# Experts' rows and results turned by VectorE in 32x32 blocks, and three five-way branches an expert

## The chip, the cores and the metric

The kernel runs on one core of one Trainium2 chip. The core has a matrix engine (TensorE, PE in the profile, its weight loads PEld), three engines that work on tiles (VectorE or DVE, ScalarE or ACT, GpSimd or POOL) and SyncE (SP), which here only issues transfers. A tile in SBUF has 128 partitions; products land in eight PSUM banks of 512 float32 columns. The metric is the device time of one execution in microseconds (us); lower is better.

## What is computed

```python
# delta rule: B, H, S, D = 4, 8, 768, 48
for t in range(S):
    kt, vt, bt = (k_n[:, :, t], v[:, :, t], beta[:, :, t, None])
    y[:, :, t] = np.einsum('bhd,bhde->bhe', q[:, :, t], state)
    v_old = np.einsum('bhde,bhd->bhe', state, kt)
    state = state + bt[:, :, :, None] * np.einsum('bhd,bhe->bhde', kt, vt - v_old)
...
x = y.transpose(0, 2, 1, 3).reshape(3072, 384)
# experts: E = 8, F = 1024
expert_idx = token_ids * np.int64(2654435761) % np.int64(E)
for e in range(E):
    mask = expert_idx == e
    h = np.maximum(x[mask] @ w1[e], 0.0)
    out[mask] = h @ w2[e]
```

`k_n` is `k` divided by its norm. All inputs and results are float32. The ids of this case give the eight experts 364, 389, 385, 423, 360, 376, 420 and 355 rows.

## The kernel before

**First phase.** The sequence is cut into 24 chunks of 32 steps (`NU`). VectorE inverts a triangular matrix for four chunks at a time (`invert`, L527 and L529), TensorE carries the state from chunk to chunk (`ks`, `ys`, `w`, `s`, `ym`), ScalarE empties PSUM. The finished rows go to `x_scratch` in DRAM with `store_x`, on SP's queue. On the same queue `spread_t` distributes the inverse to a block-diagonal tile `TB`; `spread_m`, on GpSimd's queue, does so for `MB`. The order of all work is written out by hand: `inv.do(us)` and `route.do(us)` let a generator of small VectorE operations run on for about so many microseconds between two steps, and `route.products()` lets it emit its PE products.

**Routing** (`routing`, a generator) runs beside the last eight chunks. It counts ranks with two products (L277, L278), gives every row a slot, compares slots with all positions (`hi`, `lo`, `hv`) and finds with 24 products (L382) which row sits in which slot: `gx` holds row numbers for reading, `gidx` for writing, `wid_i` for each expert which of five widths (360, 376, 392, 408, 424) holds its rows.

**Second phase.** For each expert, `gather` (an indirect transfer on GpSimd's queue, L104) fetches four tiles of 106 rows. `turn` transposes each with three products against the identity and a copy. `gemm1` forms the eight blocks of 128 hidden columns from three products each, `gemm2` the three blocks of 128 output columns from eight each. `put` transposes the result back in four pieces (L925), copies it and scatters it (L929). A float32 product is two passes of PE, so the profile counts two instructions for each.

The widths enter through a switch: `choose` (L875) branches on PE into one of five bodies that differ in the number of rows alone. An expert has two: `rows` over the first four blocks of `gemm1`, and `cols` over the whole `gemm2`. Between them lie the fifth block at the full 424 rows, 24 transposes (the results of the expert before and the rows of the one after) and the last three blocks at 424 rows. A switch can be announced ahead (`hint`, L954): `cols` is announced before the transposes, `rows` right after `cols` of the expert before. Expert 0 has no switch.

```python
                gemm1(i, xT, h_sb, arms[e], range(4), f"rows{e}")
                if e + 1 < E:
                    arms[e + 1] = arm(e + 1)
                gemm1(i, xT, h_sb, ALL, range(4, 5))
                if e + 1 < E:
                    hint(e, "cols")
```

`arm` (L950) loads the next expert's width into a register of PE. For the first expert the rows of the first 21 chunks (`x_early`) are gathered while the last chunks still run: three tiles of rows (`KE = 3`) early, the fourth when all rows are stored. Weights: expert 0's on ScalarE's queue, those of 1 and 2 on GpSimd's, later ones on SP's. A loop over overflow blocks at the end has no iteration with these ids.

Of the kernel before, what the change touches and what calls it, by code (L numbers as in the profile page):

```python
# [19 lines left out]
def kernel(  # L20
# [25 lines left out]

    KT = 4
    KE = 3
    TS = 106
    TD = 112  # L50
    CAP = KT * TS
# [9 lines left out]
    x_early = x_dram[0:CE * C * B]  # L61
# [7 lines left out]
    gx = keep.tile([P, NHI], I32)  # L69
    ov_i = keep.tile([P, NOV + 1], I32)  # L70
# [8 lines left out]
    def load_w(e, eng, i=None, dyn=None):  # L79

        i = e % 3 if dyn is None else i
        s1 = moe_w1[e] if dyn is None else moe_w1[bass.ds(dyn, 1)].rearrange("o d f -> (o d) f")
        s2 = moe_w2[e] if dyn is None else moe_w2[bass.ds(dyn, 1)].rearrange("o f d -> (o f) d")
        for co in range(CO):
            yield
            eng.dma_start(out=W1s[i][:, co], in_=s1[co * P:(co + 1) * P])
        for fo in range(0, FO, 2):
            yield
            eng.dma_start(out=W2w[i][:, fo:fo + 2],
                          in_=s2[fo * P:(fo + 2) * P].rearrange("(o p) d -> p o d", p=P))  # L90
# [12 lines left out]
    def gather(src, idx, xg):  # L103
        nc.gpsimd.indirect_dma_start(  # L104
            out=xg[0:TD], out_offset=None, in_=src,
            in_offset=bass.IndirectOffsetOnAxis(ap=idx[0:TD], axis=0),
            bounds_check=src.shape[0] - 1, oob_is_err=False)
# [10 lines left out]
    with ExitStack() as phase1:  # L118
# [101 lines left out]
        def routing():  # L220
# [12 lines left out]
            for b in range(B):  # L233
# [10 lines left out]
            nc.gpsimd.memset(cont[:, :, 0:1], 0.0)  # L244
            iota_f = rt.tile([P, P], F32)
# [51 lines left out]
                            scalar2=float(KE * TS), op0=ALU.mult, op1=ALU.add)  # L297
# [11 lines left out]
            for n in WIDTHS[1:-1]:  # L309
# [17 lines left out]
                            scalar2=float(E * KT * P - CAP - (KT - 1) * (P - TS)), op0=ALU.mult,  # L327
                            op1=ALU.add)
# [8 lines left out]
            yield 0.65  # L337
            slot = rt.tile([P, NTC], F32)
            V.tensor_reduce(slot, rank.rearrange("p e c -> p c e"), axis=AX.X, op=ALU.add)

            yield 1.0
            col = rt.tile([P, NTC], F32)
            V.tensor_scalar(out=col, in0=slot, scalar1=float(TS), scalar2=None, op0=ALU.is_ge)
            for i in range(2, KT):
                V.scalar_tensor_tensor(out=col, in0=slot, scalar=float(TS * i), in1=col,
                                       op0=ALU.is_ge, op1=ALU.add)
            V.scalar_tensor_tensor(out=slot, in0=col, scalar=float(P - TS), in1=slot,
                                   op0=ALU.mult, op1=ALU.add)
# [32 lines left out]
            for i in range(NTC):  # L381
# [11 lines left out]
            V.scalar_tensor_tensor(out=gx, in0=row, scalar=-1.0, in1=none, op0=ALU.add,  # L393
                                   op1=ALU.add)

            yield 1.2
            row_p = rt.tile([P, 3, NHI], I32)
# [9 lines left out]
            V.tensor_tensor(gidx, row, none, op=ALU.add)  # L407
# [128 lines left out]
        class Work:  # L536

            def __init__(self, it):
                self.it = it
                self.next = next(it, None)  # L540
                self.owed = 0.0

# [8 lines left out]
            def products(self):  # L551
                if self.next == "PE":
                    self.next = next(self.it, None)
# [233 lines left out]
        rt = rt_stack.enter_context(tc.tile_pool(name="rt", bufs=1, side="right"))  # L787
        w_parts = load_w(0, nc.scalar)
# [3 lines left out]
        xg0 = [XTs[1][:, i * DIN:i * DIN + DIN] for i in range(KT)]  # L792
        for c in range(NU - 2 * GC, NU + 1):
            first, last = c == NU - 2 * GC, c % GC == GC - 1
            if c < NU:
                if not last:
# [6 lines left out]
            if c < NU:  # L803
# [6 lines left out]
                if c == NU - 3:  # L810
                    route.do(3.0)
                elif c == NU - 2:
                    route.do(None)
                w(c, 0)
                if c == NU - GC:
                    assert route.next == "PE"
                    route.products()
# [5 lines left out]
            if c < NU:  # L823
# [5 lines left out]
                if c == NU - 2:  # L829
                    assert route.next == "PE"  # L830
                    route.products()
                ym(c, 0)
                y_out(c, 0)
                inv, us = invert_b(c)
                inv.do(us)
                if c >= NU - GC - 1:
                    route.do(None if c >= NU - 2 else 2.0 if c < NU - GC else 4.0)
                w(c, 1)
            if c == NU - 2:
                for kt in range(KE):  # L840
                    gather(x_early, gx[:, kt:kt + 1], xg0[kt])
# [4 lines left out]
    with tc.tile_pool(name="m_xg", bufs=8) as m_xg, \  # L846
         tc.tile_pool(name="m_h", bufs=2) as m_h, \
         tc.tile_pool(name="m_y", bufs=1) as m_y, \
         tc.tile_pool(name="m_o", bufs=5) as m_o:

        xTs = [t[:, :CO * CAP].rearrange("p (c n) -> p c n", c=CO) for t in XTs]

        yTs = [m_y.tile([P, CO, CAP + TD - TS], F32, name=f"yT{i}") for i in range(2)]
        for t in yTs:
            nc.vector.memset(t[:, :, CAP:], 0.0)
# [5 lines left out]
        ROWS = [4, 5, 6, 7, 0, 4, 5, 6]  # L861
        COLS = [7, 2, 3]
        ALL = slice(0, CAP)

        def copy(eng, out, in_):
            (nc.scalar.copy if eng is nc.scalar else nc.vector.tensor_copy)(out, in_)  # L866

        def turn(xg, xT, col, width, kt, eng):
            xT_ps = banks[2 + kt % 2][:, :CO * P].rearrange("p (c n) -> p c n", c=CO)
            for co in range(CO):  # L870
                nc.tensor.transpose(xT_ps[:, co, :width], xg[:width, co * P:(co + 1) * P],  # L871
                                    ident[:width, :width])
            copy(eng, xT[:, :, col:col + width], xT_ps[:, :, :width])

        def choose(cols, name):  # L875
# [3 lines left out]
            else:  # L879
                for i in tc.Switch({mybir.EngineType.PE: cols}, len(WIDTHS), hint=name):  # L880
                    yield slice(0, WIDTHS[i])

        def gemm1(i, xT, h_sb, cols, fos=range(FO), name=None):
            for part in choose(cols, name):
                for fo in fos:
                    for co in range(CO):
                        nc.tensor.matmul(banks[ROWS[fo]][:, part],  # L887
# [3 lines left out]
                    if part is cols:  # L891
                        relu(h_sb, fo, cols)
            if part is not cols:
                for fo in fos:
                    relu(h_sb, fo, ALL)

        def relu(h_sb, fo, cols):
            h, h_ps = h_sb[:, fo, cols], banks[ROWS[fo]][:, cols]
# [5 lines left out]
        def gemm2(i, h_sb, yT, cols, cos=range(CO), name=None):  # L904

            def take(co, part):
                copy((nc.scalar, nc.vector)[co % 2], yT[:, co, part], banks[COLS[co]][:, part])

            for part in choose(cols, name):
                for co in cos:  # L910
                    for fo in range(FO):
                        nc.tensor.matmul(banks[COLS[co]][:, part],  # L912
                                         lhsT=W2w[i][:, fo, co * P:(co + 1) * P],
                                         rhs=h_sb[:, fo, part], start=(fo == 0),
                                         stop=(fo == FO - 1))
                    if part is cols:
                        take(co, part)
            if part is not cols:
                for co in cos:
                    take(co, ALL)  # L920

        def put(yT, col, width, idx, kt, alone, eng):
            o_ps = banks[1 - kt % 2]
            for co in range(CO):
                nc.tensor.transpose(o_ps[:width, co * P:(co + 1) * P], yT[:, co, col:col + width],  # L925
                                    ident)
            o_sb = m_o.tile([P, DIN], F32, name="o_sb")
            copy(eng, o_sb[:width], o_ps[:width, :DIN])
            scat = nc.gpsimd.indirect_dma_start(  # L929
                out=out[:, :], out_offset=bass.IndirectOffsetOnAxis(ap=idx[:width], axis=0),  # L930
                in_=o_sb[:width], in_offset=None, bounds_check=N - 1, oob_is_err=False)
# [4 lines left out]
        xgs = {(0, kt): xg0[kt] for kt in range(KT)}  # L936

        def fetch(e):
            for kt in range(KT):
                xgs[e, kt] = m_xg.tile([P, DIN], F32, name="xg")  # L940
                gather(x_dram, gx[:, e * KT + kt:e * KT + kt + 1], xgs[e, kt])

        def turn_one(e, kt):
            turn(xgs.pop((e, kt)), xTs[e % 3], kt * TS, TS, kt, (nc.scalar, nc.vector)[kt % 2])

        def put_one(e, kt):
            put(yTs[e % 2], kt * TS, TD, gidx[:, e * KT + kt:e * KT + kt + 1], kt, True,
                (nc.vector, nc.scalar)[kt % 2])
# [5 lines left out]
        def hint(e, name):  # L954
            tc.switch_hint({mybir.EngineType.PE: arms[e]}, len(WIDTHS), f"{name}{e}")

        def new_h():
            return m_h.tile([P, FO, CAP], F32, name="h_sb")


        gather(x_dram, gx[:, KE:KT], xg0[KE])
        for kt in range(KE):
            turn_one(0, kt)
        for _ in load_w(1, nc.gpsimd):
            pass

        for i in range(8):
            nc.vector.memset(m_xg.tile([P, DIN], F32, name="xg"), 0.0)
        fetch(1)
        for _ in load_w(2, nc.gpsimd):  # L970
            pass


        arms = {}
        for e in range(E):
            h_sb, i, xT = new_h(), e % 3, xTs[e % 3]
            if e == 0:
                gemm1(i, xT, h_sb, slice(0, KE * TS))
                arms[1] = arm(1)
                turn_one(0, KE)  # L980
                gemm1(i, xT, h_sb, slice(KE * TS, CAP))
# [86 lines left out]
```

## Time and profile before

| what | us |
|---|---|
| three runs | 566.9, 995.24, 563.8 |
| their median | 566.9 |
| the profiled execution | 566.48 |
| its span | 564.9 |
| granted clock, mean | 0.938 |
| PE from 300 to 520 us | 219.7 of 220 busy |
| VectorE from 300 to 520 us | 30.6 of 220 busy |

The profiled execution is 1.6 us longer than its span and stands 0.4 us below the median. One of the three runs was far off the other two.

How to read the page: part 1 gives busy time, share of the span and number of instructions for each engine. Part 2 cuts the span into 40 equal slices of 14.1 us; each digit is the busy share in tenths, and the clock row gives the share of full speed granted to PE. The chain that ended last names, from each instruction back, what released it. A line such as `341.39 1.97 PE psK L887 x6` in it gives start, duration, engine, tile, source line and count. "issue" is time in which an engine waited for nothing that the profile shows. A name with a trailing q (`PEldq`, `SPq`) is the engine's sequencer or queue.

### The profile page before, as it was taken

The page shows a single profiled execution, that of the slowest core. Times are in us where ns is not written, and L with a number is a line of the kernel's source. Part 1 is how long each engine was busy: PE and PEld are TensorE (multiplying, and loading weights), DVE is VectorE, ACT ScalarE, POOL GpSimd, SP SyncE. Part 2 cuts the span into 40 slices and gives each one's busy share as a digit, 9 for nine tenths or more (in the row PEclk, how much of TensorE's full clock was granted, in tenths as well). Part 3 has the DMA queues.
Part 4 walks back from the last instruction along what each step waited for, and adds up shares of the span by engine and source line. Part 5 has one row for each costly group of instructions (what it writes and reads, how often), then busy time and mean ns, then how long its engine had stood idle before and what let it go on. Part 6 is the DMA issues. An engine that isn't in the chain of part 4 may idle for free.

```text
span 564.9 us, 14221 instructions
## 1 busy us (share of the span) xinstructions
PE 516.4 (91%) x5596; PEld 385.8 (68%) x5596; DVE 264.9 (47%) x707; ACT 205.7 (36%) x448; POOL 255.9 (45%) x409
## 2 busy tenths in 40 slices
PE   8969798889898878988999999999999999999993
PEld 7858788888788777976675656555566565655572
DVE  6899987998989988396310201102011020200200
ACT  5857575887787523353110202102011020200100
POOL 9608676878878785673672320504105020110202
PEclk9659897999999977599999999999999999999998
DMA  6926576888688495574698153631436310010101
GB/s 107 183 56 102 105 144 112 148 133 157 123 153 147 75 177 121 110 167 103 214 364 242 43 158 112 193 119 54 150 115 192 124 44 3 11 34 3 48 0 40
DMA packets 130282, 66.22 MB, mean 117 GB/s; under 512 B 112856, under 2 KB 120114, under 8 KB 130176
## 3 DMA queue, kind: packets, MB, share of 16 engines
q1 hardware_dynamic: 113328, 33.12, 28.3%
q0 software_dynamic: 15328, 28.39, 20.3%
q10 hardware_dynamic: 1520, 3.15, 1.8%
q8 instruction: 85, 1.39, 1.1%
q14 instruction: 21, 0.17, 0.1%
HBM read 49.67 MB, written 10.22 MB: 106 GB/s over the span
## 4 chain that ended last, share of the span: by engine, by line
PE 51%; issue 0%; ACT 0%; DVE 0%; POOL 0%; POOLq 0%
PE psT L912 15%; PE psS L887 9%; PE psS L912 8%; PE psK L887 6%; PE psW L887 6%; PE psG L887 3%; PE psT L871 2%; PE psG L925 1%; PE psY L925 1%; POOL out_dram L929 0%; ACT xT L866 0%; PE psG L629 0%; PE psG L599 0%; DVE o_sb L866 0%; ACT h_sb L900 0%
## 5 line engine op out<-in xcount | busy, mean ns | idle before, releaser
L929 POOL DMA_INDIRECT out_dram<-o_sb,gidx x32 | 30.5, 953 | 203.7 <-DVE o_sb L866 179.1
L912 PE MATMUL psT<-h_sb,w 128*128 128x424 f32 (+5 forms) x288 | 88.8, 466 | 0.0
L912 PEld LDWEIGHTS psT<-h_sb,w 128*128 128x128 f32 x288 | 52.3, 190 | 35.1 <-issue 15.9
L175 POOL DMA_DIRECT2D K<-in_k_dram x96 | 55.6, 585 | 43.1 <-PE psS L618 36.1
L529 DVE TENSOR_TENSOR U<-U,tmp 128x31 f32<-128x31 f32 (+15 forms) x186 | 63.8, 343 | 6.4
L527 DVE TENSOR_TENSOR tmp<-U,Ni 128x31 f32<-128x31 f32 (+15 forms) x186 | 63.4, 341 | 5.3
L563 POOL DMA_DIRECT2D MB<-MT x96 | 55.5, 584 | 4.4 <-PE psG L629 1.3
L181 POOL DMA_DIRECT2D V<-in_v_dram x96 | 55.5, 584 | 3.4 <-DMA V<-in_v_dram 1.8
L887 PE MATMUL psS<-xT,w 128*128 128x424 f32 (+5 forms) x162 | 52.2, 467 | 0.0
L606 PE MATMUL psW<-R,TB 128*64 128x48 f32 x736 | 35.0, 237 | 13.1 <-DVE R L591 6.9
L464 PE MATMUL psG<-sd,w 96*64 96x64 f32 x640 | 30.4, 245 | 17.3 <-ACT sd L443 11.8
L618 PE MATMUL psS<-W,K 128*96 128x96 f32 x368 | 44.1, 267 | 1.2 <-ACT W L612 1.2
L912 PE MATMUL psS<-h_sb,w 128*128 128x424 f32 (+5 forms) x144 | 45.1, 466 | 0.0
L612 ACT ACTIVATE W<-psW 64x192 f32<-64x192 f32 x96 | 31.2, 324 | 36.1 <-PE psW L606 34.7
L451 ACT ACTIVATE w<-psT,own 96x512 f32<-96x512 f32 x66 | 43.2, 689 | 0.4
L887 PEld LDWEIGHTS psS<-xT,w 128*128 128x128 f32 x162 | 29.5, 190 | 19.9 <-issue 10.9
L866 DVE COPY yT<-psT 128x424 f32<-128x424 f32 (+2 forms) x9 | 5.0, 551 | 80.7 <-PE psT L912 80.7
L618 PEld LDWEIGHTS psS<-W,K 128*96 128x96 f32 x368 | 39.2, 179 | 3.0 <-ACT W L612 1.4
L606 PEld LDWEIGHTS psW<-R,TB 128*64 128x64 f32 x736 | 30.0, 151 | 15.7 <-DVE R L591 10.4
L464 PEld LDWEIGHTS psG<-sd,w 96*64 96x64 f32 x640 | 26.0, 156 | 20.9 <-ACT sd L443 14.8
L912 PEld LDWEIGHTS psS<-h_sb,w 128*128 128x128 f32 x144 | 26.2, 190 | 17.8 <-issue 9.1
L887 PE MATMUL psK<-xT,w 128*128 128x424 f32 (+5 forms) x108 | 36.6, 475 | 1.5 <-DVE xT L866 0.7
(203 smaller groups left out, 795.6 us busy)
## 6 DMA issues: line engine op xcount, KB each, us to landing
w<-in_moe_w_dram SPq DMA_DIRECT2D x15, 512.0 KB
w<-in_moe_w_dram SPq DMA_DIRECT2D x20, 384.0 KB
Kd<-in_k_dram SPq DMA_DIRECT2D x24, 192.0 KB
Qd<-in_q_dram SPq DMA_DIRECT2D x24, 192.0 KB
K<-in_k_dram POOLq DMA_DIRECT2D x96, 48.0 KB, 2.9
V<-in_v_dram POOLq DMA_DIRECT2D x96, 48.0 KB, 3.6
x_scratch<-x_sb SPq DMA_DIRECT2D x96, 48.0 KB
TB<-TU SPq DMA_DIRECT2D x96, 32.0 KB
```

The costliest lines, as they stand in the source:

```text
L175: nc.gpsimd.dma_start(out=K4s[c % 3][quarter(i), :, i % 2, :], in_=k_r[i, c * C:(c + 1) * C])
L181: nc.gpsimd.dma_start(out=Vs[c][quarter(i)], in_=v_r[i, c * C:(c + 1) * C])
L451: nc.scalar.activation(to[:, :, :, r], psT, ACT.Copy, scale=own[:, r:r + 1])
L464: nc.tensor.matmul(psG[pair(p), hg, j, ks], lhsT=KT[:, j, hg, p].rearrange("p r s -> p (r s)"), rhs=sd[:, j, ks, 2 * hg + p], start=True, ...
L527: V.tensor_tensor(tmp, U[:, j:j + 1, 0:n].to_broadcast([P, m, n]), Ni[:, j, j + 1:, None].to_broadcast([P, m, n]), op=ALU.mult)
L529: V.tensor_tensor(U[:, j + 1:, 0:n], U[:, j + 1:, 0:n], tmp, op=ALU.add)
L563: eng.dma_start(out=dst[quarter(i), :, i, :], in_=src[quarter(i)])
L606: nc.tensor.matmul(psW[pair(p), i], lhsT=TBs[c % 2][:, HT * h + i, 2 * p:2 * p + 2].rearrange("k r t -> k (r t)"), rhs=Rs[h][:, i], start= ...
L612: nc.scalar.activation(Ws[h][pair(p), :, p], psW[pair(p)], ACT.Copy)
L618: nc.tensor.matmul(psS[h][:, i], lhsT=K4s[c % 3][:, HT * h + i], rhs=Ws[h][:, i], start=(c == 0 and i == 0), stop=True, skip_group_check=True)
L887: nc.tensor.matmul(banks[ROWS[fo]][:, part], lhsT=W1s[i][:, co, fo * P:(fo + 1) * P], rhs=xT[:, co, part], start=(co == 0), stop=(co == CO ...
L912: nc.tensor.matmul(banks[COLS[co]][:, part], lhsT=W2w[i][:, fo, co * P:(co + 1) * P], rhs=h_sb[:, fo, part], start=(fo == 0), stop=(fo == ...
```

## The change

- **Rows in quarters.** A row of 384 values becomes four quarters of 96. Partition `32*a + j` of a tile holds quarter `a` of the row in place `j` of a 32-row block. VectorE's transpose, which turns every 32x32 block in place, then gives the operand of `gemm1` directly, and one more turns each output block back. For that the weights are read differently: W1 with input `3*p + c` on partition `p`, W2 with every third column (`co::CO`).
- **Where the rows come from.** Experts 1 to 7: `fetch` gathers four whole tiles of 128 rows, `spread_rows` rearranges them with 16 small transfers on SP's queue, `rows_in` turns all 14 blocks with one instruction. Expert 0: 14 gathers of quarters (`KE = 9` blocks early, five late), with indices `x4`.
- **Results.** `rows_out` turns the three PSUM banks and issues 14 scatters of quarters with indices `g4`, in place of four scatters of rows. The last expert's results are still transposed by PE, in four pieces, of which two follow the last product.
- **Three switches an expert**: `top` (blocks 0 to 3), `low` (4 to 7) and `cols`; all are announced inside `choose`, directly ahead. Expert 0 has `cols` too. PSUM banks go round in turn (`take_banks`).
- **Routing** drops the three-step column count, adds two groups of four small products (`by_quarter`), and is spread over chunks 17 to 22: its first products come at the end of chunk 19 and not in chunk 20, its second after `w(22, 0)`.
- **Queues.** Weights of experts 1 and 2 move from GpSimd's to SP's queue. `spread_t` of chunk 17 is issued ahead of the loads of the ids.

```diff
-    KE = 3
-    TS = 106
-    TD = 112
-    CAP = KT * TS
+    KE = 9
+    T = 32
+    QD = DIN // 4
+    CAP = 424
+    NB = -(-CAP // T)
...
-            eng.dma_start(out=W1s[i][:, co], in_=s1[co * P:(co + 1) * P])
+            eng.dma_start(out=W1s[i][:, co], in_=s1.rearrange("(p c) f -> c p f", c=CO)[co])
...
+            yield "PE"
+
+            def by_quarter(idx, n):
+                ps = bank(ps_t, "t")[:, :4 * n].rearrange("p (m k) -> p m k", m=4)
+                for m in range(4):
+                    nc.tensor.matmul(ps[:, m], lhsT=sel[:, m].rearrange("p a j -> p (a j)"),
+                                     rhs=idx[:, 0:n], start=True, stop=True)
+                return ps.rearrange("p m k -> p k m")
+
+            ps = by_quarter(gx_f, KT)
+            yield 0.2
+            V.tensor_scalar(out=x4, in0=ps, scalar1=4.0, scalar2=quarter_f[:, 0:1], op0=ALU.mult,
+                            op1=ALU.add)
...
+        spread_t(NU - 2 * GC + 1)
         w_parts = load_w(0, nc.scalar)
...
-                if c == NU - 3:
-                    route.do(3.0)
-                elif c == NU - 2:
-                    route.do(None)
+                if c >= NU - GC:
+                    route.do(3.5 if c < NU - 2 else None)
                 w(c, 0)
-                if c == NU - GC:
-                    assert route.next == "PE"
-                    route.products()
+                if c == NU - 2:
+                    route.products(2)
...
             if c == NU - 2:
-                for kt in range(KE):
-                    gather(x_early, gx[:, kt:kt + 1], xg0[kt])
+                for m in range(KE):
+                    gather(x_early, x4.rearrange("p k m -> p (k m)")[:, m:m + 1], xq0[:, m])
+                route.products(4)
...
             if isinstance(cols, slice):
                 yield cols
             else:
+                tc.switch_hint({mybir.EngineType.PE: cols}, len(WIDTHS), name)
                 for i in tc.Switch({mybir.EngineType.PE: cols}, len(WIDTHS), hint=name):
                     yield slice(0, WIDTHS[i])
...
+        def rows_in(xT, xq, ms):
+            nc.vector.transpose(
+                xT[:, :, T * ms.start:T * ms.stop].rearrange("p c (m j) -> p m c j", j=T),
+                xq[:, ms].rearrange("p m (i c) -> p m c i", c=CO))
+
+        def rows_out(e, ps):
+            oq = m_o.tile([P, NB, QD], F32, name="oq")
             for co in range(CO):
+                nc.vector.transpose(oq[:, :, co::CO],
+                                    ps[co][:, :CW].rearrange("p (m j) -> p m j", j=T))
+            for m in range(NB):
+                scatter(out_quarters, g4[:, e].rearrange("p k m -> p (k m)")[:, m:m + 1],
+                        oq[:, m])
...
+        def spread_rows(e):
+            xqs[e] = m_xq.tile([P, KT * 4, QD], F32, name="xq")
+            xg = xgs.pop(e)
+            to = xqs[e].rearrange("p (k m) f -> p m k f", m=4)
+            for m in range(4):
+                n = len(range(m, NB, 4))
+                for a in range(4):
+                    nc.sync.dma_start(out=to[T * a:T * a + T, m, :n],
+                                      in_=xg[T * m:T * m + T, :n, QD * a:QD * a + QD])
...
             if e == 0:
-                gemm1(i, xT, h_sb, slice(0, KE * TS))
-                arms[1] = arm(1)
-                turn_one(0, KE)
-                gemm1(i, xT, h_sb, slice(KE * TS, CAP))
+                gemm1(i, xT, h_sb, slice(0, KE * T), range(FO))
+                arms[0] = arm(0)
+                rows_in(xT, xq0, late)
+                gemm1(i, xT, h_sb, slice(KE * T, CAP), range(FO))
             else:
-                gemm1(i, xT, h_sb, arms[e], range(4), f"rows{e}")
-                if e + 1 < E:
-                    arms[e + 1] = arm(e + 1)
-                gemm1(i, xT, h_sb, ALL, range(4, 5))
-                if e + 1 < E:
-                    hint(e, "cols")
-            if e + 2 < E:
-                fetch(e + 2)
-
-            for kt in range(KT):
-                if e > 0:
-                    put_one(e - 1, kt)
-                if e + 1 < E:
-                    turn_one(e + 1, kt)
+                rows_out(e - 1, done.pop(e - 1))
+                gemm1(i, xT, h_sb, arms[e], range(4), f"top{e}")
+            if e + 1 < E:
+                arms[e + 1] = arm(e + 1)
             if e > 0:
-                gemm1(i, xT, h_sb, ALL, range(5, FO))
+                if e + 2 < E:
+                    fetch(e + 2)
+                gemm1(i, xT, h_sb, arms[e], range(4, FO), f"low{e}")
             if e + 1 < E:
-                if e == 0:
-                    gemm2(i, h_sb, yTs[0], ALL)
-                else:
-                    gemm2(i, h_sb, yTs[e % 2], arms[e], name=f"cols{e}")
-                hint(e + 1, "rows")
+                rows_in(xTs[(e + 1) % 3], xqs.pop(e + 1), slice(0, NB))
+                done[e] = take_banks(CO)
+                gemm2(i, h_sb, arms[e], done[e], name=f"cols{e}")
```

## The prediction, made before the changed kernel was run

> **What bounds the kernel now.** I read, in this order: busy shares and slices of the page, the chain that ended last, the sequencer's records of line 1063 (the dispatch of each switch), the granted clock by stretch, GpSimd's timeline at the seam of the two phases.
>
> ```profile
> PE 516.4 (91%) x5596; PEld 385.8 (68%) x5596; DVE 264.9 (47%) x707; ACT 205.7 (36%) x448; POOL 255.9 (45%) x409
> PE   8969798889898878988999999999999999999993
> PEclk9659897999999977599999999999999999999998
> ```
>
> From about 268 us (slice 19 on) TensorE (PE) is never idle: the expert phase costs exactly what PE is given. The chain for expert 2 (its first four blocks, one full-width block, the transposes, the other three):
>
> ```profile
> 341.39 1.97 PE psK L887 x6
> ...
> 349.29 2.14 PE psG L887 x6
> 351.43 0.33 PE psY L925 x3
> ...
> 353.79 0.27 PE psT L871 x3
> 354.06 2.16 PE psK L887 x6
> ```
>
> So 24 PE transposes lie in the chain from 351.43 to 354.06, 2.63 us, and each later block is charged at 424 rows: 2.13 us, where the arm of 392 takes 1.97.
>
> What covers a branch decides the rest. The sequencer's dispatches, of all switches, then entry, exit and the second entry of expert 2:
>
> ```profile
> L1063 PEldq COMPARE_BRANCH  x26: 305/2412/4424, 300.8 to 519.0; - x26
> L1063 PEldq COMPARE_BRANCH  x1: 3807/3807/3807, 336.6 to 336.6; - x1
> L1063 PEldq COMPARE_BRANCH  x1: 3508/3508/3508, 343.2 to 343.2; - x1
> L1063 PEldq COMPARE_BRANCH  x1: 404/404/404, 354.2 to 354.2; - x1
> ```
>
> Columns are minimum, median and maximum in ns and first and last start. The entry of `rows`, hinted just before, holds the sequencer 3.8 us (336.6 to 340.4); leaving that short body takes 3.5 us; the entry of `cols`, hinted 6 us earlier, 0.4 us. PE doesn't notice the first, because the sequencer runs about 5 us ahead (336.6 against the end of the matrix product at 341.39). Once it does:
>
> ```profile
> 446.09 0.27 issue
> 446.36 2.15 PE psK L887 x6
> ```
>
> That entry took 4.42 us. And what an idle PE costs, two stretches of the first phase:
>
> ```profile
> 205.00:218.00 13.00, 11.81 (x166) 11.19 (x168) 10.36 (x27) 2.94 (x8) 7.18 (x13) 0.50 0.60 118
> 225.00:239.00 14.00, 12.88 (x164) 11.85 (x164) 5.19 (x18) 3.59 (x10) 8.57 (x15) 0.51 0.56 109
> ```
>
> The seventh figure is the granted clock, 0.50: PE's own timeline has an idle 2.59 us up to 205.88 and 2.79 us up to 226.12.
>
> [...] the instruction queue moved 85 packets of 1.39 MB (16 KB each), and entries hinted only just before cost 2.1 us (first arm) to 4.4 us. [...] No operand of the kernel before shows a 12-byte stride into PE. [...] the trace has one of 1024 elements at 1.23 us (L500), 1.99 with a strided output (L532).
>
> **Part by part**, against the profiled execution's 566.5 us (span 564.9; the median shown is 566.9, so no correction).
>
> *PE transposes leave.* Experts 1 to 6: 6 x 2.64 (351.43 to 354.06 and its like) = 15.8. Expert 7: 526.78 to 529.03, waits included, 2.25. Expert 0's are in the seam below. Gain 18.1.
>
> *Widths.* From the arms in the trace (392, 392, 424, 360, 376, 424, 360 for experts 1 to 7) blocks 4 to 7 save 4 x (2.13 - 1.98, 1.98, 2.13, 1.81, 1.89, 2.13, 1.81): 0.6+0.6+0+1.3+1.0+0+1.3 = 4.8. Expert 0's second product goes to its arm, 376 by the reference's ids: 48 passes x (0.356 - 0.316) = 1.9. The last one, split 256+168 instead of 324+100: a pass costs 0.84 ns a row (318 rows: 0.267), but 100 rows cost 0.110, a floor; 48 x (0.2725 + 0.110 - 0.215 - 0.141) = 1.3. Gain 8.0.
>
> *Routing and the seam.* Order on VectorE: the first work moves under chunks 17 to 19, whose VectorE wait (idle 5.70 before 240.20) swallows it; the four `lo` compares (3.56) move ahead of chunk 22. The slots' 24 products start some 2.5 us earlier, but then come four small products and one more VectorE step, so I find the first index about where it is:
>
> ```profile
> 258.96 1.09 POOL L104 DMA_INDIRECT xT<-x_scratch,gx  x1 [3.00 <-DVE row_p L398]
> ...
> 272.26 0.99 POOL L104 DMA_INDIRECT xT<-x_scratch,gx  x1 [9.58 <-issue]
> ```
>
> Instead of three gathers nine follow, one every 1.33 us (start to start): the ninth starts at 269.4, lands 3.0 later (median for xT), VectorE turns 864 elements in 1.1: first product at about 273.3, where it now starts at 268.08. PE's last chunk ends near 267: idle 6 us, clock halved. The five late gathers (from 272.3: the last lands at 281, turned by 282) stay under the first 11.6 us product. Both products: 48 x (288 rows 0.242 + 136 rows 0.114) = 17.1, so expert 0's second product begins at 290.4, against 289.39 now: loss 1.0, before the clock. A bound on both sides: an index 3 us earlier gives -2, later +5. Moving `spread_t` ahead of the id loads on SP removes a 1 us wait for TB at 206; the VectorE queue holds R until 205 all the same: gain 1.0.
>
> *Moved off PE at no cost, and their cover.* VectorE: one turn of 1344 elements (1.6 to 2.6) and three of 448 from PSUM (0.5 to 0.9 each) an expert, beside four relus of 0.6: under 8 of 32 us. Its relus queue behind the three output turns, but these are over 3 us into an 8 us block. GpSimd: 14 scatters instead of 4, at 1.25 each 17.5, then four gathers (5.3): 23 of 32 us. SP: 16 spreads at 0.61 = 9.8, behind gathers that land 7 us after issue, and weights behind them; the rows are due a whole expert later. First time tightest: rows for expert 1 turned near 306, due near 314. If that cover is gone, PE waits the difference.
>
> *The new branch.* `low` stands right behind `top`: leaving `top`, loading the next width and entering `low` lie in one line, with only `top`'s 8 us to cover them. Expert 2 with the durations shown: left at 346.7, width and registers to 348.05, dispatch at 348.4, entry 3.8: 352.3, but `top` ends at 349.29: PE idle 3.0. The same sum for experts 1 to 7, arm for arm (first arm 2.1 to 2.4; the others 3.8 to 4.4): 3.1, 3.0, 1.6, 2.1, 4.6, 0, 1.1 = 15.5. `low` to `cols`, which loses its early hint, without the width load: 2.3, 2.2, 0.9, 1.3, 4.1, 0 = 10.8. Expert 0 into its new switch: behind passes of 0.114 the sequencer is 1.8 us ahead, needs 5.7: 3.9. Loss 30.2.
>
> *The clock.* Halved stretches after the start lasted 3.4 us (61.5 to 64.9), 6.8 (88.8 to 95.6) and twice over 13 (above), 9.4 in the mean; half of it is lost: 4.7 us each. Idle of 2 us or more is likely at the seam and in experts 0, 1, 2, 5, perhaps 4: 5.7 of them, 26.8; a halved PE then covers the second entry: -7. Loss 19.8, between 0 (clock held) and 32 (all at 6.8).
>
> *Tail.* Two scatters instead of one after the last product, 1.25 apart: loss 1.3.
>
> Sum: 566.5 - 18.1 - 8.0 + 1.0 - 1.0 + 1.3 + 30.2 + 19.8 = 591.7: **592 us**.
>
> **Unknown both ways:** weights at a 12-byte stride in the second product. A load takes 190 ns under passes of about 330: unseen at up to 1.7 times, +19 us if doubled (50 ns x 48 x 8), a gain excluded since it adds no bandwidth. I take nothing.
>
> **Rivals.** (1) *Entries stay hidden*, because `low`'s first arm lies just behind the exit and its block is already there: no stall, no halving after the seam. 591.7 - 30.2 - 19.8 + 4.7 (the seam's halving stays) = 546, faster. For it: the exits of `cols` cost 0.3 us. Against: entering `rows` right behind such an exit cost 2.1 to 4.4 every time. It turns where exit, width and entry together fall under 8 us. (2) *Stalls, but the clock holds*: 572, range 565 to 578. For it: one slice at 0.63 busy was not punished; against: the two stretches above. (3) *Weight loads bind as well*: 592 + 19 = 611. That the change is not what it says is excluded: the order of instructions shows three switches an expert and no transposes in experts 0 to 6.
>
> **Numbers.** Forecast 0.57 (578 to 606), hidden entries 0.13, clock holds 0.21, weight loads or a later seam 0.09. The range 563 to 612 leaves out the hidden case and the far end. A measurement of this kernel tells about 2% (11 us): faster 0.13, same 0.20 (most of the second rival), slower 0.67.
>
> **What would show it.** Right: idle PE named issue between two L923 groups and before L945, entries of 2 to 4.4 us twice an expert, clock near half in slices of the expert phase, first L923 near 273. Wrong: entries under 0.5 us, PE idle nowhere after 275, or a clock of 1.0 throughout; a weight load over 300 ns would make the third rival.

## The result and the profile after

| | median, us | range, us | executions | profiled, us | span, us | granted clock |
|---|---|---|---|---|---|---|
| before | 565.35 | 560.28 to 995.24 | 4 | 566.48 | 564.9 | 0.938 |
| after | 608.3 | 605.56 to 613.91 | 4 | 605.56 | 604.0 | 0.915 |

The ratio, which leaves out the one execution of 995.24 us, is 1.0805, 95% interval 1.0675 to 1.0934: the change makes the kernel slower. The forecast was 592 in a range of 563 to 612.

The page of the kernel after, the same rows as were shown of before:

```profile
PE 506.9 (84%) x5432; PEld 397.9 (66%) x5432; DVE 278.2 (46%) x700; ACT 186.3 (31%) x405; POOL 327.5 (54%) x479
PE   7967988988988698979788688899969968999990
PEclk9569899999999958879889799898979979999996
```

PE has 164 instructions fewer and is busy 9.5 us less, in a span that is 39.1 us longer. From slice 19 on the row of PE was all nines before; now sixes to eights stand among them, and the clock row dips beside them. So the time went into idle PE and half clock, not into work. The sequencer's records of all switches, then top entry, top exit, `low` entry, `low` exit and `cols` entry of expert 2 (ns minimum, median, maximum; first and last start):

```profile
L1121 PEldq COMPARE_BRANCH  x42: 310/3358/6647, 288.9 to 562.3; - x42
L1121 PEldq COMPARE_BRANCH  x1: 6186/6186/6186, 352.0 to 352.0; - x1
L1121 PEldq COMPARE_BRANCH  x1: 3325/3325/3325, 360.5 to 360.5; - x1
L1121 PEldq COMPARE_BRANCH  x1: 3555/3555/3555, 365.5 to 365.5; - x1
L1121 PEldq COMPARE_BRANCH  x1: 3582/3582/3582, 371.3 to 371.3; - x1
L1121 PEldq COMPARE_BRANCH  x1: 4254/4254/4254, 375.8 to 375.8; - x1
```

That is 21 us in branches within 28 us (352.0 to 380.1). The trace's instruction queue moved ten blocks of 16 KB in that time, one or two of them in each of the five branches, and at least one in each of the 31 branches over 2 us of the whole trace (112 blocks in all, 85 before); a branch of this length is called a fetch below. What PE makes of it, in its own timeline of that expert (start, duration, operation; in brackets the idle time before it and what released it):

```profile
358.48 4.19 PE L923 MATMUL psS<-xT,w 128*128 128x392 f32 x12 [1.63 <-DVE oq L959]
...
364.48 2.14 PE L923 MATMUL psY<-xT,w 128*128 128x392 f32 x6
369.23 4.21 PE L923 MATMUL psT<-xT,w 128*128 128x392 f32 x12 [2.61 <-issue]
...
375.25 2.14 PE L923 MATMUL psW<-xT,w 128*128 128x392 f32 x6
380.31 2.01 PE L945 MATMUL psS<-h_sb,w 128*128 128x392 f32 x4 [2.91 <-issue]
```

Three stalls, one for each entry. The first is put down to VectorE, but the entry that began at 352.0 and took 6.19 us ended at 358.2, just ahead of the block, while VectorE's last turn there ended at 357.7: it is a fetch too. Stalls over 0.7 us between 292 and 568 us, summed by the entry that they stand at: `top` 3.9 (experts 1, 2), `low` 19.6 (experts 1 to 5, 7), `cols` 12.4 (experts 1, 2, 4, 5), 35.9 together, and 3.12 more at expert 0's `cols`. The clock, in three stretches (the columns are the length, then busy time of PE, PEld, DVE, ACT and POOL, the granted clock, the share of DMA and GB/s):

```profile
352.00:359.00 7.00, 5.37 (x17) 3.68 (x17) 1.18 (x2) 0.00 (x0) 0.99 (x1) 1.00 1.02 364
446.25:453.10 6.85, 4.18 (x7) 2.52 (x8) 0.00 (x0) 0.18 (x1) 5.02 (x7) 0.50 0.16 56
482.00:489.00 7.00, 0.58 (x2) 0.38 (x2) 0.60 (x1) 0.00 (x0) 5.31 (x6) 0.87 0.99 360
```

The second is one of seven halved stretches of the expert phase (four of 3.4 us, three of 6.8: 34 us, half of it lost: 17 at most, since PE stood idle in 5 of the 34). The first and third are the two entries of over 6 us in experts 2 and 5: the DMA share was 1.02 and 0.99 while the sequencer fetched. That was not in the forecast.

The end, by the drain of GpSimd's queue, kernel before:

```profile
L1063 POOLq DRAIN  x3: 50/108/2107, 562.0 to 564.6; - x3
```

and after:

```profile
L1121 POOLq DRAIN  x3: 50/103/7339, 595.8 to 603.7; - x3
```

The last drain grew by 5.2 us, though the last scatter had landed at 591.8.

### The profile page after: what moved, and what is told of

Its sections match the earlier page's. It is cut to its first block, busy times and chain, and to the rows that moved or that the text cites. A ratio compares the mean times of both kernels' runs of the same rounds, so it can differ in the third digit from the quotient of the medians.

```text
span 604.0 us, 14287 instructions
## 1 busy us (share of the span) xinstructions
PE 506.9 (84%) x5432; PEld 397.9 (66%) x5432; DVE 278.2 (46%) x700; ACT 186.3 (31%) x405; POOL 327.5 (54%) x479
## 5 line engine op out<-in xcount | busy, mean ns | idle before, releaser
L966 POOL DMA_INDIRECT out_dram<-oq,g x98 | 96.6, 986 | 160.1 <-DVE oq L959 132.3
L183 POOL DMA_DIRECT2D K<-in_k_dram x96 | 55.6, 585 | 34.2 <-PE psS L649 27.7
L923 PE MATMUL psT<-xT,w 128*128 128x392 f32 (+5 forms) x108 | 36.7, 489 | 11.3 <-issue 11.3
L637 PE MATMUL psW<-R,TB 128*64 128x48 f32 x736 | 33.6, 233 | 12.3 <-DVE R L622 11.9
L945 PE MATMUL psT<-h_sb,w 128*128 128x424 f32 (+2 forms) x96 | 37.0, 545 | 6.2 <-issue 6.2
L945 PE MATMUL psS<-h_sb,w 128*128 128x392 f32 (+4 forms) x128 | 35.8, 438 | 5.2 <-issue 5.2
L923 PE MATMUL psS<-xT,w 128*128 128x392 f32 (+5 forms) x108 | 33.9, 461 | 3.7 <-issue 1.9
L923 PEld LDWEIGHTS psT<-xT,w 128*128 128x128 f32 x108 | 20.3, 199 | 25.1 <-issue 18.4
L945 PEld LDWEIGHTS psT<-h_sb,w 128*128 128x128 f32 x96 | 24.7, 260 | 18.3 <-issue 10.3
L945 PEld LDWEIGHTS psS<-h_sb,w 128*128 128x128 f32 x128 | 29.0, 258 | 11.6 <-issue 7.9
L619 PE MATMUL psK<-S,w 96*64 96x48 f32 x736 | 33.0, 233 | 0.0
```

Source lines behind the costliest of these rows:

```text
L183: nc.gpsimd.dma_start(out=K4s[c % 3][quarter(i), :, i % 2, :], in_=k_r[i, c * C:(c + 1) * C])
L637: nc.tensor.matmul(psW[pair(p), i], lhsT=TBs[c % 2][:, HT * h + i, 2 * p:2 * p + 2].rearrange("k r t -> k (r t)"), rhs=Rs[h][:, i], start= ...
L923: nc.tensor.matmul(ps[fo][:, part], lhsT=W1s[i][:, co, fo * P:(fo + 1) * P], rhs=xT[:, co, part], start=(co == 0), stop=(co == CO - 1))
L945: nc.tensor.matmul(ps[co][:, part], lhsT=W2w[i][:, fo, co::CO], rhs=h_sb[:, fo, part], start=(fo == 0), stop=(fo == FO - 1))
L966: scat = nc.gpsimd.indirect_dma_start(out=dst, out_offset=bass.IndirectOffsetOnAxis(ap=idx, axis=0), in_=o_sb, in_offset=None, bounds_chec ...
```

## The experiments

The theory, from expert 2 above: every switch costs the sequencer two fetches (6.19 and 3.33 us at `top`); with nothing between two switches these exceed its lead over PE (1.1 us at `low`, dispatched at 365.5 while `top` ran to 366.6), PE idles (2.61 us at `low`, 2.91 at `cols`), and after idle time the clock is halved (0.50 from 446.25 to 453.10 us). The rivals: VectorE's turns or the row transfers are late; the strided weights slow PE; the fetch is lengthened by the weight loads.

### Taking one switch away, or all

```diff
+                tc.switch_hint({mybir.EngineType.PE: arms[e]}, len(WIDTHS), f"cols{e}")
-                gemm1(i, xT, h_sb, arms[e], range(4, FO), f"low{e}")
+                gemm1(i, xT, h_sb, ALL, range(4, FO))
```

> The kernel after with `low` removed: blocks 4 to 7 stand inline at 424 rows, and the hint for `cols` is issued ahead of them (for expert 0 ahead of the late rows' half). Theory (three switches in a row starve PE): of the 35.9 + 3.1 us of idle PE behind 292 us about 5 stay (at the entries of `top`, behind the long second product), at most two of seven half-clock stretches stay, blocks 4 to 7 cost 4.8 more: 605.6 - 34 - 13 + 5 = 563, between 557 and 568. Rival, VectorE's turns or the row transfers hold PE: its idle stays, above 595. Rival, the strided weight loads slow PE: they stay as well, so about 605 + 5.

Measured: 561.5 us, 0.9971 of before (0.9945 to 0.9998). PE's timeline of expert 2:

```profile
339.90 4.11 PE L924 MATMUL psS<-xT,w 128*128 128x392 f32 x12
...
347.81 4.43 PE L924 MATMUL psT<-xT,w 128*128 128x424 f32 x12
...
354.21 2.30 PE L924 MATMUL psW<-xT,w 128*128 128x424 f32 x6
356.41 1.95 PE L946 MATMUL psS<-h_sb,w 128*128 128x392 f32 x5
```

No bracket is left: PE never idles. One stall over 0.7 us remains behind 290 us (2.79 at expert 1's `top`, whose entry took 6.95), and the clock is full from 272 to 541. The stretch from expert 0's second product to expert 7's takes 229.6 us (288.86 to 518.48) against 246.05 before and 275.26 after: here is the gain that VectorE's turns should bring. With 36 us less stalled and 17 less halved, against the 4.8 us that blocks 4 to 7 cost more at 424 rows, the third branch with its neighbours explains 48 of the 48.9 us between the two profiled executions. The edit gives `cols` both inline cover and an earlier hint. Its records separate them in part: at experts 1, 2 and 5 the entry of `cols` still took 3.55, 5.70 and 3.68 us, and PE idled at none of them, so there the inline blocks were the cover; the other four took 0.35 to 0.42 us. Expert 2's:

```profile
L1125 PEldq COMPARE_BRANCH  x1: 5695/5695/5695, 350.5 to 350.5; - x1
```

The relus followed their blocks by at most 0.3 us; this matters below.

In no_switch every product runs at 424 rows.

> The kernel after with no switch at all, all widths 424. Theory: no idle of PE over 0.7 us between 292 us and expert 7's end, clock full there, widths cost 9.7 (first products) + 6.9 + 1.9 (second products) = 18.5 more: 605.6 - 39 - 17 + 18.5 = 568, between 564 and 572. Rival, turns or transfers hold PE: PE idles at the first block or the second product of experts all the same, above 600. Rival, strided weight loads: passes of 424 rows above 0.356 us, time above 580.

Measured: 569.6 us, 1.0126 of before (1.0096 to 1.0156). The whole stretch between the two second products, columns as above:

```profile
292.70:531.90 239.20, 239.20 (x675) 148.60 (x674) 46.44 (x56) 14.65 (x28) 115.26 (x117) 1.00 0.41 135
```

PE is busy 239.20 us of 239.20 at full clock, so turns and row transfers hold it nowhere in this stretch. The instruction queue moved 44 blocks, against 87 in two_switches and 112 in after. And 16 passes of the second product at 424 rows take as long with strided weights, here, as without, in the kernel before:

```profile
509.12 5.86 PE L945 MATMUL psK<-h_sb,w 128*128 128x424 f32 x16
```

```profile
500.12 5.86 PE L912 MATMUL psS<-h_sb,w 128*128 128x424 f32 x16
```

The first two rivals fall, as far as these products go. Against two_switches it is 9.6 us longer, which is what the remaining two switches bring.

### Adding the switch to the kernel before

```diff
-                gemm1(i, xT, h_sb, ALL, range(4, 5))
+                hint(e, "low")
+                gemm1(i, xT, h_sb, arms[e], range(4, FO), f"low{e}")
                 if e + 1 < E:
                     hint(e, "cols")
```

The last three blocks at 424 rows, behind the transposes, go.

> The kernel before with one thing added, a switch `low` of five widths over blocks 4 to 7, hinted directly ahead, right behind `rows`; the PE transposes then follow, with the hint for `cols` ahead of them. Theory: each of seven new entries directly behind a short body leaves PE idle 0 to 5 us, some 15 us in the sum, and three to five halved stretches of 1.7 to 4.7 us; widths give back 4.8 (less the 0.3 a block that the covered relus cost): before + 10 to + 25 us. Rival, a hint directly ahead is enough: before - 5.

Measured: 616.4 us, 1.0924 of before (1.0853 to 1.0994), +54: the direction of the theory, more than twice its size. PE's timeline at the end of expert 2's first product:

```profile
375.76 0.44 PE L871 MATMUL psT<-ident,xg 106*128 106x106 f32 x3
381.67 2.97 PE L912 MATMUL psS<-h_sb,w 128*128 128x392 f32 x4 [5.47 <-issue]
```

This stall is at `cols`, which was hinted ahead of the transposes. Six entries of `low` cost 15.1 us of idle; five of `cols` cost 22.5 more (5.43, 5.47, 4.50, 3.52, 3.56) at experts 1, 2, 3, 5 and 6. There the inline blocks that had stood between leaving one switch and entering the next are gone, and the entries themselves took 3.75 to 5.89 us where the kernel before shows 0.31 to 2.86; the run doesn't separate the two. Together 37.6, and half of 44 us of halved clock is 22: 37.6 + 22 - 4.8 for widths = 54.8. So the branch alone, without anything else of the change, makes the kernel before slower by more than the whole change did: it also takes away cover of the next switch.

### Are the fetches lengthened by the weight loads?

No loads for experts 3 to 7 (the loop over `load_w(e + 3, nc.sync)` is dropped).

> The kernel after without the weight loads of experts 3 to 7, which use the weights of experts 0, 1, 2 again (so their output rows differ); nothing else is changed. Theory that the instruction fetch shares the DMA engines with these loads: the entries and exits of 6.2 to 6.65 us fall to 4.5 or less, PE's idle behind 292 us falls from 39 to some 20 to 25 us, time 575 to 592. Rival, the entry takes as long as its cold fetch whatever else moves: entries of over 6 us stay, time 603 to 610.

Measured: 588.7 us, a single execution. The entries of 6.19 (expert 2's `top`), 6.57 (expert 3's `low`) and 6.65 us (expert 5's `low`) became 4.32, 3.51 and 3.83. Two exits had been as long: 6.33 us (expert 1's `low`) and 6.28 (expert 4's `top`) became 3.30 and 3.88. The first and the third entry in the sequencer's records:

```profile
L1118 PEldq COMPARE_BRANCH  x1: 4319/4319/4319, 348.8 to 348.8; - x1
...
L1118 PEldq COMPARE_BRANCH  x1: 3832/3832/3832, 468.1 to 468.1; - x1
```

and the window around the first, with a DMA share of 0.07 in place of 1.02:

```profile
348.00:355.00 7.00, 7.00 (x23) 5.03 (x22) 1.57 (x2) 0.00 (x0) 0.16 (x1) 1.00 0.07 12
```

Expert 1's `top`, beside the loads that stayed, still took 6.53. Idle fell from 39.0 to 28.4 us (20 to 25 was expected), halved clock from 34.2 to 20.4: 10.6 + 6.9 = 17.5, against 16.8 measured between the two profiled executions. The contention is real, 2 to 3 us for a fetch that meets a load, and it is the smaller part: without it most entries still take 2.3 to 4.6 us.

### The strided weights and the drain

```diff
-                        nc.tensor.matmul(ps[co][:, part], lhsT=W2w[i][:, fo, co::CO], rhs=h_sb[:, fo, part],
+                        nc.tensor.matmul(ps[co][:, part], lhsT=W2w[i][:, fo, co * P:(co + 1) * P], rhs=h_sb[:, fo, part],
```

> The kernel two_switches with the weights of the second product read without the stride of 3 (`co*P:(co+1)*P` in place of `co::CO`); the 384 columns of the result then come out in another order, all else is the same. Theory that a strided weight load costs only where it is longer than the pass beside it: loads fall from 255 to 190 ns, passes of 360 to 424 rows stay, the 168-row passes of expert 7 fall from 0.16-0.18 to 0.14 us: 1.4 us less than two_switches (561.5), so 560. Rival, the stride slows every pass: 144 passes at 30 to 60 ns, 4 to 9 us less, 553 to 557.

Measured: 606.6 us, 1.0622 of before (1.0518 to 1.0725), not to be read against 561.5: relus came late in this run (next part). Its own rows answer the question. In two_switches, the weight loads of one bank of the second product (ns minimum, median, maximum) and, in PE's timeline, the 168-row passes of expert 7:

```profile
L946 PEld LDWEIGHTS psK<-h_sb,w x48: 250/251/253, 329.0 to 502.0; 128*128 128x128 f32 x48
```

```profile
528.84 2.91 PE L946 MATMUL psW<-h_sb,w 128*128 128x168 f32 x16
...
532.24 5.80 PE L946 MATMUL psS<-h_sb,w 128*128 128x168 f32 x32
```

and in w2_plain:

```profile
L946 PEld LDWEIGHTS psK<-h_sb,w x48: 186/190/190, 348.6 to 552.6; 128*128 128x128 f32 x48
```

```profile
579.45 2.44 PE L946 MATMUL psW<-h_sb,w 128*128 128x168 f32 x16
...
582.38 4.73 PE L946 MATMUL psS<-h_sb,w 128*128 128x168 f32 x32
```

The load falls from 251 to 190 ns, the 48 short passes from 8.71 to 7.17 us; 16 passes of 376 and of 424 rows stay at 5.22 and 5.86 us. That is 1.5 us where 1.4 was expected, and no more: a stride of 12 bytes makes a load 1.32 times as long, and only the passes shorter than the load show it (149 ns without the stride at 168 rows; 326 and 366 ns at 376 and 424).

In few_scatters `rows_out` issues no scatter for experts 0 to 5 (`range(NB if e > 5 else 0)`).

> The kernel two_switches without the 84 scatters of experts 0 to 5 (their rows of the output are not written); their transposes stay. Theory that GpSimd's last drain grows with the number of scatters: 18 remain of 102, the drain falls from 7.34 to 2 us or less, and INC_SWDGE_SEM from 1.97 to 0.7 or less; 6 us less than two_switches, 555.5. Rival, the drain is a fixed cost of this program: 7.3 stays, time 560 to 562.

Measured: 572.0 us, 1.0045 of before (1.0007 to 1.0084). The drain:

```profile
L1125 POOLq DRAIN  x3: 46/103/7174, 567.7 to 575.8; - x3
```

7.17 us with 18 scatters, 7.34 with 102: the rival is right, the drain doesn't grow with their number. What sets it stays open.

### Relus that come late

Two attempts at something better ran in the same session as the last two:

> The kernel after, its three switches kept, but no two of them next to each other: `top` has blocks 0 to 2, block 3 follows inline at 424 rows, `low` has blocks 4 to 6, block 7 inline; the hint of each next switch stands ahead of the inline block. Theory (a switch is free where its hint has some 4 us and the exit before it has its body): entries of `low` and `cols` fall to 0.3-1 us, two or three idles stay, two blocks at 424 rows cost 2.4 against after and 2.4 less than two_switches: 559 to 566. Rival, three switches an expert cost whatever stands between them, since leaving each needs a fetch too: idle of PE above 20 us, 580 or more.

> The kernel two_switches with five blocks in `top` and three inline, and expert 0's late rows turned on VectorE between blocks 5 and 6 of the early half instead of behind all its relus. Theory: a fifth block at its own width saves 1.2, the idle 1.36 us at 282 goes, and the 6.4 us of three inline blocks still cover leaving `top` and entering `cols`: 2.5 less than two_switches, 559. Rival, the cover is now too short: PE idles 1 to 3 us at each `cols`, 565 to 580.

Measured: 605.1 to 616.4 us for spaced and 606.0 us for best1 (1.0604, 1.0495 to 1.0712). Both are far off, and so was w2_plain, whose edit leaves relus and their waits alone. A third attempt, and two of the programs once more:

> The kernel best1 with no switch over expert 1's first product (all its blocks at 424 rows). In the last four runs ScalarE's and VectorE's relus came up to 9 us behind PE's blocks, in every kernel, and a sixth of the trace's records is missing, which no run before showed; so best1 is asked again. Theory: against two_switches (561.5) a fifth block at its own width saves 1.2, the late rows turned earlier 1.4, and expert 1's entry of 6.9 us, which left PE idle for 2.8, costs 0.6 of rows instead: 561.5 - 4.8 = 556.7; relus within 0.3 us of their blocks. Rival, three inline blocks are too little cover for leaving `top` and entering `cols`: PE idles 1 to 3 us at each `cols`, 563 to 578.

> The kernel spaced once more, unchanged, since its first run had relus up to 9 us late at every product. Theory as before (an inline block with the hint ahead of it is cover enough): entries of `low` and `cols` 0.3-1 us or hidden, 559 to 566. Rival, two entries and two exits within one first product can't be covered by 17 us of matmuls: PE idles over 20 us in the sum, 580 or more.

> The kernel two_switches once more, unchanged. Six kernels run since then, five of them with nearly its structure, took 572 to 613 us, with relus of ScalarE and VectorE 2 to 9 us behind PE's blocks. Theory that this came with the conditions of those two sessions and not with their edits (which touch neither relus nor their waits): this kernel gives either 561 with relus prompt, if the conditions are those of its first run, or some 600 with late relus, if they are not. Rival, the edits caused it: 561 and prompt relus in any conditions, also where the kernel before reads 566 to 570.

Measured: 606.0 (1.0714, 1.0665 to 1.0764), 611.3 (1.0779, 1.0727 to 1.0832) and, for the very program that had taken 561.5, 612.9 (1.0777, 1.0681 to 1.0872). So the attempts say nothing on their edits against 561.5: the same program stands at two levels. Who PE waits for in two_again (total us, times, longest):

```profile
PE psS L946 <- DVE h_sb L939: 9.8, 2, 5.0
PE psK L946 <- DVE h_sb L939: 5.7, 1, 5.7
```

and the end of expert 2's first product, on PE, ScalarE and VectorE in turn:

```profile
376.26 2.30 PE L924 MATMUL psW<-xT,w 128*128 128x424 f32 x6
378.39 4.98 PE L946 MATMUL psS<-h_sb,w 128*128 128x392 f32 x14
388.11 2.33 PE L946 MATMUL psS<-h_sb,w 128*128 128x392 f32 x3 [4.74 <-DVE h_sb L939]
```

```profile
381.81 0.52 ACT L937 ACTIVATE h_sb<-psK 128x424 f32<-128x424 f32 x1 [9.09 <-PE psS L946]
```

```profile
387.46 0.60 DVE L939 TENSOR_SCALAR h_sb<-psW 128x424 f32<-128x424 f32 x1 [12.53 <-remote]
```

Block psK was done by 376.3, its relu started at 381.8; psW by 378.4, its relu at 387.5, though VectorE had been idle for 12.5 us. One stretch of SyncE's weight loads in two_again is delayed too (minimum, median, maximum ns):

```profile
L97 SPq EVENT_SEMAPHORE  x20: 3/17/701, 336.6 to 484.1; - x20
```

All 20 of these semaphore steps took 17 ns in two_switches; here three in a row, between 336 and 343 us, took 0.70 us each. And the trace holds 13,093 semaphore updates where the first run of this program has 15,516; nearly all that are missing are records of DMA landings (11,295 against 13,661). Seven of the eight runs from w2_plain on lack 15 to 16% of what their like hold (few_scatters can't be compared); before, after and the first four experiments don't. The chip isn't the difference: two_switches, with prompt relus, and w2_plain, with late ones, both ran on chip 12, and the late runs are spread over four chips. Lost records and late engines came together; no run shows whether one brings the other or another disturbance brings both, and every execution here was recorded, so none shows the program without recording. What is shown: without most of the scatters the lateness goes, since few_scatters, in the same session as w2_plain and best1 at 606, had prompt relus from expert 1 on and took 572. The kernel before was hit little (566 to 570 in those sessions, 562.5 in that of two_switches).

> The kernel after once more, unchanged, since two_switches took 561 us at first and 613 on another chip later, with relus up to 9 us behind PE's blocks. If relus are prompt (the kernel before then at 560 to 565): 605 to 614 again. If they are late: theory that the switches' stalls and the late relus hit different moments, so that they add: 640 to 660. Rival, PE waits at the same places for both, so that one hides the other: 608 to 625.

Measured: 622.1 us, 1.1006 of before (1.0939 to 1.1073), with late relus. The rival is right: PE waits at the same places for both, one hides the other. So the third branch costs 47 us (608.3 against 561.5) where relus are prompt, and 9 (622.1 against 612.9) where they are late, each read across two sessions. Of the kernels with the new row handling, after is the slowest in either case.

None of the attempts beats both kernels reliably: two_switches does it by 0.3% at best. Whether an inline block between switches is enough (spaced) and whether five blocks in `top` gain their 1.2 us (best1, best2) stays open.

## Why the prediction was right, point by point

The mechanism was the forecast one, and the sign with it; the median stands 16 us above the 592. The forecast's terms against the profiled execution (+39.1 us of span):

| term | forecast | measured |
|---|---|---|
| PE transposes and widths, without the last product | -24.8 | -24.0 (two_switches: 229.6, less 2.8 idle, less an estimated 4.8 for the widths of `low` that it lacks, against 246.05) |
| stalls at `low` | +15.5 | +19.6 |
| stalls at `cols`, experts 1 to 6 | +10.8 | +12.4 |
| stall at expert 0's `cols` | +3.9 | +3.1 |
| stalls at `top` | 0 | +3.9 |
| clock | +19.8 | +18.7 (17.0 in the expert phase, 1.7 ahead) |
| last product, its passes alone | -1.3 | +0.4 |
| end (transposed pieces, scatters, drain) | +1.3 | +6.3 |
| seam and `spread_t` | 0 | -1.8 |

The measured column sums to 38.6 of 39.1.

- **Branch stalls: right in kind, mis-sized.** 30.2 was forecast, 39.0 came. The step that was too small is the price of a fetch: entries at "the others 3.8 to 4.4" and exits at 3.5, from a kernel whose fetches met less traffic (DMA share 0.66 at most while they ran). With a DMA share near 1 three entries behind expert 1 took 6.2 to 6.65 and two exits 6.3, which no_w_loads brought back to 3.3 to 4.3. Expert by expert the terms miss by more than their sums: `low`, forecast at 3.1, 3.0, 1.6, 2.1, 4.6, 0 and 1.1 for experts 1 to 7, came to 1.9, 2.6, 2.2, 5.3, 6.4, 0 and 1.2; `cols`, at 2.3, 2.2, 0.9, 1.3, 4.1 and 0 for experts 1 to 6, to 6.0, 2.9, 0, 1.2, 2.3 and 0. The two long exits stand ahead of the two largest misses, expert 1's `cols` and expert 4's `low`. For the same reason the entries of `top`, which I left at nothing, stalled twice.
- **Clock: right in the sum, by luck in the pieces.** I took 5.7 stretches of 9.4 us, less 7 us of cover; seven of 3.4 to 6.8 came in the expert phase and one of 3.4 at the seam. More and shorter stretches happened to add up to nearly the same loss.
- **Last product.** I gave strided loads no cost because passes of about 330 ns hide them, and priced the split into 256 and 168 rows by rows alone. The passes took 18.7 us where 17.1 was forecast (18.4 before). The 168-row passes are shorter than the load: 1.5 us of the difference, by w2_plain. The third rival's 300 ns, an estimate that no load in the trace of before showed, was not reached (251).
- **End.** The two scatters were counted, not the drain behind them, 5.2 us longer.
- **Seam.** The first gather began at 253.0, 6 us earlier than I took it, and the first product at 268.57 against the forecast 273.3 (by its own spacing of 1.33 us the ninth gather would start at 269.6, not 269.4, and the product at 273.7). In exchange the late rows' turn, which I saw covered, stood behind expert 0's relus in VectorE's queue until 282.58 and left PE idle for 1.36 us.
- **Moved work.** VectorE's turns, GpSimd's scatters and SP's spreads are hidden where relus are prompt (no_switch: PE busy for 239.20 of 239.20 us). That cover is not robust: with late relus the scatters are, by few_scatters (572.0 us, against 606.6 for w2_plain in the same session), the part of the change that hurts.
- **Rivals.** Hidden entries (546) and a clock that holds (572) fall by the trace of after: it has the stalls and the halved stretches. The third, weight loads that bind, holds for the 168-row passes alone.

## What to carry to other kernels

Price a branch by both of its fetches, entry and exit (up to 6.65 and 6.33 us in after), at the DMA load of that moment, and against the work that lies between it and the next branch: a third branch with nothing between saved 4.8 us of rows and cost some 50. Inline work between two branches was worth keeping here, even though it computes padding. Where several engines hand over in short steps, measure the program on more than one occasion before a gain of a few per cent is believed.

## What was not expected of the hardware

- Entering a branch that is announced directly ahead took 2.3 to 4.6 us in the kernel after where the DMA share was under 0.6, and 6.2 to 6.95 (the longest in two_switches) where weight loads held it near 1 (0.94 to 1.04 in after). Leaving one took up to 3.8 us, or 6.3 beside such loads.
- Between 60 us and the last product of before and after, halved clock came in pieces of 3.4 us: 3.4, 6.8 and 13.65 occurred. Idles of 2.19, 2.30 and 2.91 us in after were followed by one; those of 2.61 there and of 2.79 in two_switches were not.
- A weight load at a 12-byte stride takes 251 ns (two_switches) in place of 190 (w2_plain).
- GpSimd's last drain took 7.34 us in after, two_switches, no_switch, no_w_loads and two_again, all with the new row handling, 7.17 with 84 scatters fewer, and 2.11 in before and before_low, with the old one; in after it ended at 603.2, although the last scatter had landed at 591.8.
- One program took 561.5 us in one session and 612.9 in another, the kernel before 562.5 and 567.6 beside it.
